# Normalising and transposing four tiles of x in pairs, and moving two pairs of transposes behind a gate and up piece

## The chip, the cores and the metric

The kernel runs on one core of one Trainium2 chip. The metric is device time in microseconds (us) of one execution, median of several. All arithmetic is float32; matrix products are made from float32 values that are split into a high part and a low remainder, three products each.

## The reference, cut to what matters

```python
xn = _layernorm(x, axis=-1)                     # x: 1 x 2048 x 640
s = _A_ref(xn, A_wqkv, A_wo)                    # q, k, v; 32 heads of 20; window of 8 keys, 2 apart; output product
g = _silu(_B_ref(xn, B_w_gate, B_w_up, B_w_down))   # ((xn Wg) * (xn Wu)) Wd, inner width 1536
return x + s * g
```

The layer norm has no weights: `(x - mean) / sqrt(var + 1e-5)` over the 640 columns of a row.

## The kernel before, in words

The 2048 rows are 16 tiles of 128 rows. Tiles 0 to 7 hold the even rows, tiles 8 to 15 the odd rows. Every product needs the normalised x transposed, in `xT`: one buffer per group of four tiles ("chunk" 0 to 3), with a high and a low part.

Tiles 0 to 7 come to it so. `moments` (L180) takes mean and variance of a tile on the vector engine (DVE): two `bn_stats` (L185) and one `bn_aggr` (L186) per tile. `rstd` (L189) makes the scale: a square root on ScalarE (ACT, L191), then a reciprocal and a correction step on DVE. For one or two tiles it works tile by tile (L194 per tile, L195, then L199, L200, L201 per tile); for more tiles it works on all of them at once (L194, L195, L203 to L206). `apply` (L209) subtracts and scales in place, one DVE instruction per tile. `trans` (L218) then makes five 128x128 transposes on TensorE (PE, L223), four into one PSUM bank and one into another; ACT copies each bank out as the high part (L224), and DVE takes the low part from the same bank (L225).

Tiles 8 to 15 have their moments taken from one layout of x (into `mvo`); their scales are made together by `rstd(mvo..., mro...)`; `spread` (L236) distributes means and scales over the partitions with four products `q<-mro,sel` on PE (L240) and one ACT copy (L241). The same x is loaded again in another layout (`load_xq`, L234) into the space of the first, and `trans_odd` (L249) applies norm and transpose on DVE.

`qkv(u, i)` (L283) is one tile's product with one group of heads, 15 matmuls with 300 columns (L292) and two ACT copies. `gate_up(f, ch)` (L384) is one piece of the gated part: 15 matmuls of 512 columns into a bank of tag g, an ACT copy `gs` (L394), 15 into a bank of tag u, and then, as long as no attention is running, an ACT copy `hs` (L407), a GpSimd (POOL) product (L408) and a store. A callback in `amid` is issued between the gate and the up matmuls. Tags g and u have two banks each, tag q has four; the first piece (0,0) is made in two halves of 256 columns.

Nothing reorders the work: the order in which the program records instructions is the order of each engine's queue, and the framework adds the semaphore waits. The order around the change is that of lines 664 to 685: `norm(4, 4)`, `qkv(0, 2)`, `qkv(0, 3)`, the second half of piece (0,0), `trans(4)`, `trans(5)`, `moments(8, 2)`, piece (1,0) with `trans(6)` between gate and up, `moments(10, 2)`, the load of tiles 8 to 11 in the second layout, `trans(7)`, a weight load, `qkv(0, 4)`, `qkv(0, 5)`, `moments(12, 2)`, `moments(14, 2)`, two more loads, the scales of the odd tiles, and piece (0,1) with `spread` between gate and up. On DVE the instructions of these steps stand in just this order; the same holds for ACT. Loads and stores all go through the queue of SyncE (SP).

Of the kernel before, what the change touches and what calls it, by code (L numbers as in the profile page):

```python
# [50 lines left out]
def kernel(  # L51
# [23 lines left out]
    def st(shape, tag, bufs, dt=F32):  # L75
        cnt[0] += 1
        return sb.tile(shape, dt, tag=tag, bufs=bufs, name=f"{tag}_{cnt[0]}")

    def pt(shape, tag, bufs):
        cnt[0] += 1  # L80
        return ps.tile(shape, F32, tag=tag, bufs=bufs, name=f"{tag}_{cnt[0]}")
# [37 lines left out]
    def load_wf(f):  # L119
        wf_raw[f] = st([P, KD, 2, P], "wraw", 3)  # L120
        nc.sync.dma_start(wf_raw[f], wgu[f])
# [49 lines left out]
    def xT_tile(s):  # L171
        if s % TPC == 0:
            y = st([P, 2, KD, CH], "xc", NCH, F32R)
            xT.append((y[:, 0], y[:, 1]))
        hi, lo = xT[s // TPC]
        c = (s % TPC) * P
        return hi[:, :, c:c + P], lo[:, :, c:c + P]


    def moments(s0, n, mv=None):  # L180
        stats = st([P, n, 2, 6], "stats", 2)
        mv = st([P, n, 2], "mv", 2) if mv is None else mv
        for i in range(n):
            for a in range(2):
                nc.vector.bn_stats(stats[:, i, a, :], xt[s0 + i][:, a * HALF:(a + 1) * HALF])  # L185
            nc.vector.bn_aggr(mv[:, i, :], stats[:, i])  # L186
        return mv

    def rstd(var, out, n):  # L189
        r = st([P, 4, NE], "rstd", 2)[:, :, :n]  # L190
        nc.scalar.activation(r[:, 0, :], var, AF.Sqrt, bias=eps_t)  # L191
        step = 1 if n <= 2 else n
        for i in range(0, n, step):
            nc.vector.tensor_scalar_add(r[:, 1, i:i + step], var[:, i:i + step], EPS)  # L194
        nc.vector.reciprocal(r[:, 2, :], r[:, 0, :])  # L195
        if step == 1:
            for i in range(n):
                ve, a, b = (r[:, k, i:i + 1] for k in (1, 2, 3))
                nc.vector.tensor_scalar(b, a, a, ve, op0=ALU.mult, op1=ALU.mult)  # L199
                nc.vector.tensor_scalar(b, b, -0.5, 1.5, op0=ALU.mult, op1=ALU.add)  # L200
                nc.vector.tensor_scalar(out[:, i:i + 1], b, a, None, op0=ALU.mult)  # L201
            return
        nc.vector.tensor_mul(r[:, 3, :], r[:, 2, :], r[:, 2, :])  # L203
        nc.vector.tensor_mul(r[:, 3, :], r[:, 3, :], r[:, 1, :])
        nc.vector.tensor_scalar(r[:, 3, :], r[:, 3, :], -0.5, 1.5, op0=ALU.mult, op1=ALU.add)
        nc.vector.tensor_mul(out, r[:, 3, :], r[:, 2, :])  # L206

    def apply(y, m, r):
        nc.vector.tensor_scalar(y, y, m, r, op0=ALU.subtract, op1=ALU.mult)  # L209

    def norm(s0, n, mv=None):
        mv = moments(s0, n) if mv is None else mv
        r = st([P, n], "r", 2)
        rstd(mv[:, :, 1], r, n)
        for i in range(n):
            apply(xt[s0 + i], mv[:, i, 0:1], r[:, i:i + 1])

    def trans(s, bank=("q", 4)):  # L218
        hi, lo = xT_tile(s)
        for k0, k1 in ((0, 4), (4, KD)):  # L220
            p = pt([P, k1 - k0, P], *(("q", 4) if k0 else bank))
            for k in range(k0, k1):
                nc.tensor.transpose(p[:, k - k0, :], xt[s][:, k * P:(k + 1) * P], ident)  # L223
            nc.scalar.activation(hi[:, k0:k1, :], p, AF.Copy)  # L224
            nc.vector.tensor_sub(lo[:, k0:k1, :], p, hi[:, k0:k1, :].bitcast(F32))  # L225
# [7 lines left out]
    def load_xq(s, n, t):  # L233
        nc.sync.dma_start(t, xq[:, s - NE:s - NE + n, :])  # L234
# [48 lines left out]
    def qkv(u, i, runs=ALL_RUNS, at=None, act=None):  # L283

        g, r = UN[u]
        c = GROUPS[g] * DH
        p = pt([P, 3 * c], "q", 4)
        t0 = (i % TPC) * P
        for n, (a, b, k) in enumerate(runs):
            if n == at:  # L290
                act()
            nc.tensor.matmul(p, xT[(r * NE + i) // TPC][a][:, k, t0:t0 + P], wq[g][b][:, k], start=n == 0,  # L292
                             stop=n == len(runs) - 1, skip_group_check=act is not None)
        nc.scalar.activation(kv_t[u][:, :, W - 1 + i, :], p[:, c:].rearrange("p (a c) -> p a c", a=2), AF.Copy)  # L294
        nc.scalar.activation(q_t[u][:, i, :], p[:, :c], AF.Copy)
        for i0, i1 in ((1, 5), (5, NE)):
            if i == i1 - 1:
                for p0, p1 in ((0, 112), (112, 127)):
                    nc.sync.dma_start(kv_t[u][p0 + 1:p1 + 1, :, i0 - 1:i1 - 1, :],
                                      kv_t[u][p0:p1, :, W - 1 + i0:W - 1 + i1, :])  # L300
# [67 lines left out]
    def advance(budget):  # L368
        credit[0] += budget
        while running and credit[0] > 0:  # L370
            try:
                credit[0] -= next(running[0][1])
            except StopIteration:
                running.pop(0)
        if not running:
            credit[0] = 0
# [4 lines left out]
    def gate_up_half(f, ch, n, p, c=slice(0, CH), **parts):  # L381
        mm3(p[:, c], [([t[:, k, n, :] for t in wf[f]], [t[:, k, c] for t in xT[ch]]) for k in range(KD)], **parts)

    def gate_up(f, ch, between=(), amid=(), part=None):  # L384
        if part is None:
            pp = [pt([P, CH], "g", 2), pt([P, CH], "u", 2)]
            c = slice(0, CH)
        else:
            pp, c = part, slice(CH // 2, CH)
        gate_up_half(f, ch, 0, pp[0], c)  # L390
        for act in amid:
            act()
        gs = st([P, CH], "gs", 2)
        nc.scalar.activation(gs, pp[0], AF.Copy)  # L394
        for act in between:
            act()
        share = (c.stop - c.start) / CH
        finish_piece()
        advance(PACE * 3.25 * share)
        gate_up_half(f, ch, 1, pp[1], c)  # L400

        def finish():
            hs = st([P, CH], "hs", 2)
            if running:
                nc.vector.tensor_mul(hs, pp[1], gs)  # L405
            else:
                nc.scalar.activation(hs, pp[1], AF.Copy)  # L407
                nc.gpsimd.tensor_mul(hs, hs, gs)  # L408
            nc.sync.dma_start(h_scr[ch * TPC:(ch + 1) * TPC, :, f, :].rearrange("t p c -> p t c"),
                              hs.rearrange("p (t c) -> p t c", c=P))  # L410

        unfinished.append(finish)
        if not running:
            finish_piece()
        advance(PACE * 3.25 * share)
# [3 lines left out]
    def finish_piece():  # L419

        while unfinished:
            unfinished.pop(0)()
# [236 lines left out]
    for i in range(NE - 1):  # L659
# [1 line left out]
    sel = st([P, NQ, P], "sel", 1)  # L661
    nc.gpsimd.tensor_copy(sel.rearrange("p q (b i) -> p q b i", i=QB),
                          ident.rearrange("p (q i) -> p q i", i=QB).unsqueeze(2).to_broadcast([P, NQ, NQ, QB]))
    norm(4, 4)
    qkv(0, 2)
    qkv(0, 3)
    gate_up(0, 0, part=part0)
    trans(4)
    trans(5)
    moments(8, 2, mvo[:, 0:2])  # L670
    gate_up(1, 0, amid=(lambda: trans(6),))
    moments(10, 2, mvo[:, 2:4])
    load_xq(8, 4, xc[:, 4:8])
    trans(7)
    load_wf(2)
    qkv(0, 4)
    qkv(0, 5)
# [188 lines left out]
```

## Time and profile before

| what | value |
|---|---|
| time, median of 3 runs | 786.98 us (786.91 to 787.13) |
| time of the profiled execution | 786.92 us |
| its span, first to last instruction | 785.0 us |
| PE matmul busy | 777.6 us, 99% |
| PE weight loads busy | 709.0 us, 90% |
| DVE busy | 661.4 us, 84% |
| ACT busy | 234.4 us, 30% |
| POOL busy | 145.5 us, 19% |

A row of the timeline reads: start in us from the beginning of the span, busy us, engine, line, operation, output tile and input tiles, shape, how many instructions are merged in the row, and in square brackets how long the engine was idle before it and what ended the idle time. PEld rows are weight loads of PE, which run beside its matmuls; SPq rows are issues in SyncE's queue. A merged row has the start of its first instruction and the summed busy time. L12 is line 12 of the kernel. Rows of a table by stretches give the stretch, its length, busy time of each engine with the number of instructions, the clock granted to PE, the share of the DMA engines' time and GB/s.

### The profile page before, as it was taken

To read this page: it belongs to the slowest core of one execution; us is meant where nothing else is said; L and a number is where in the kernel's file an instruction comes from. 1 tells how busy PE (TensorE), PEld (TensorE's weight loads), DVE (VectorE), ACT (ScalarE), POOL (GpSimd) and SP (SyncE) were. 2 spreads that over 40 slices of the span, in tenths; PEclk is the share of its full clock that TensorE was granted. 3 is DMA by queue.
4 is the path that set the end of the run, shared out by engine and by line. 5 is a ranking of instruction groups with operands and counts; after the bars stand their busy time and mean duration, and the time that the engine had idled before them with its cause. 6 is when DMAs were issued, how large, how long until landed. Compare 5 with 4: busy or idle time off the path is not lost.

```text
span 785.0 us, 11221 instructions
## 1 busy us (share of the span) xinstructions
PE 777.6 (99%) x4454; PEld 709.0 (90%) x4454; DVE 661.4 (84%) x660; ACT 234.4 (30%) x536; POOL 145.5 (19%) x110
## 2 busy tenths in 40 slices
PE   8999999999999999999999999999999999999997
PEld 6889898889898898899898989888899999999997
DVE  6989899999999979997999999991278677777775
ACT  4434211121122211311221212012366564444442
POOL 4401212022023100500231000113467600000000
PEclk9999999999999999999999999999999999999999
DMA  9162122141142221404032132332797574555534
GB/s 326 70 223 86 31 70 63 48 123 48 50 113 80 75 71 61 118 27 112 28 113 77 58 86 59 112 96 66 166 262 222 169 268 139 206 201 181 181 101 135
DMA packets 81661, 92.68 MB, mean 118 GB/s; under 512 B 23032, under 2 KB 63304, under 8 KB 81480
## 3 DMA queue, kind: packets, MB, share of 16 engines
q1 hardware_dynamic: 81608, 91.96, 37.9%
q8 instruction: 35, 0.57, 0.3%
q14 instruction: 18, 0.15, 0.1%
HBM read 54.53 MB, written 28.31 MB: 106 GB/s over the span
## 4 chain that ended last, share of the span: by engine, by line
PE 98%; ACT 1%; DMA 1%; DVE 0%; SPq 0%; issue 0%
PE q L292 27%; PE u L95 21%; PE g L95 21%; PE q L605 11%; PE q L95 9%; PE u L605 5%; PE g L605 3%; DMA wraw<-in_wqkv 1%; PE q L223 0%; ACT wf L85 0%; ACT xc L224 0%; SPq L135 0%; DVE t L209 0%; ACT wqh L85 0%; PE q L240 0%
## 5 line engine op out<-in xcount | busy, mean ns | idle before, releaser
L95 PE MATMUL u<-xc,wf 128*128 128x512 f32 (+1 forms) x735 | 176.2, 391 | 0.0
L95 PE MATMUL g<-xc,wf 128*128 128x512 f32 (+1 forms) x735 | 176.2, 391 | 0.0
L95 PEld LDWEIGHTS u<-xc,wf 128*128 128x128 f32 x735 | 135.9, 188 | 32.1
L95 PEld LDWEIGHTS g<-xc,wf 128*128 128x128 f32 x735 | 135.4, 188 | 30.8
L292 PE MATMUL q<-wqh,xc 128*128 128x300 f32 (+1 forms) x960 | 159.8, 310 | 0.9 <-ACT xc L224 0.9
L292 PEld LDWEIGHTS q<-wqh,xc 128*128 128x128 f32 x960 | 146.1, 188 | 2.9 <-ACT xc L224 1.3
L326 DVE TENSOR_TENSOR t<-q,kv 128x1600 f32<-128x1600 f32 (+1 forms) x48 | 98.8, 2058 | 9.6 <-DMA kv<-kv 9.6
L347 DVE TENSOR_TENSOR t<-e,kv 128x1600 f32<-128x1600 f32 (+1 forms) x48 | 96.9, 2037 | 1.1
L86 POOL TENSOR_TENSOR wf<-wraw,wf 128x256 fp32r<-128x256 f32 (+2 forms) x22 | 47.1, 2161 | 253.0 <-ACT wf L85 253.0
L329 DVE TENSOR_REDUCE lg<-t 128x80 f32<-128x1600 f32 (+1 forms) x48 | 92.6, 1930 | 1.2
L394 ACT ACTIVATE gs<-g 128x512 f32<-128x512 f32 x48 | 28.7, 598 | 205.8 <-PE g L95 197.2
L292 PE MATMUL q<-wql,xc 128*128 128x300 f32 (+1 forms) x480 | 86.3, 310 | 0.0
L355 DVE TENSOR_TENSOR t<-t,t 128x1600 f32<-128x1600 f32 (+1 forms) x36 | 78.6, 2184 | 1.1
L292 PEld LDWEIGHTS q<-wql,xc 128*128 128x128 f32 x480 | 74.4, 188 | 0.0
L294 ACT ACTIVATE kv<-q 128x200 f32<-128x200 f32 (+1 forms) x96 | 33.4, 348 | 135.7 <-PE q L292 135.6
L605 PE MATMUL q<-xc,wf 128*128 128x320 f32 x432 | 67.3, 309 | 0.0
L605 PEld LDWEIGHTS q<-xc,wf 128*128 128x128 f32 x432 | 64.3, 188 | 0.0
L86 POOL TENSOR_TENSOR wql<-wraw,wqh 128x300 fp32r<-128x300 f32 (+4 forms) x15 | 33.2, 2239 | 142.5 <-ACT wqh L85 142.5
L95 PE MATMUL q<-wf,wf 128*128 128x320 f32 x156 | 35.7, 311 | 0.0
L405 DVE TENSOR_TENSOR hs<-u,gs 128x512 f32<-128x512 f32 x39 | 26.6, 683 | 0.8 <-issue 0.8
L86 DVE TENSOR_TENSOR wf<-ot,wf 128x640 fp32r<-128x640 f32 x13 | 17.2, 1322 | 12.0 <-ACT wf L85 12.0
L95 PEld LDWEIGHTS q<-wf,wf 128*128 128x128 f32 x156 | 26.1, 189 | 0.0
(169 smaller groups left out, 890.8 us busy)
## 6 DMA issues: line engine op xcount, KB each, us to landing
h_scr<-hs SPq DMA_DIRECT2D x48, 256.0 KB, 2.3
wraw<-in_wgu SPq DMA_DIRECT2D x12, 640.0 KB, 4.9
t<-h_scr SPq DMA_DIRECT2D x8, 768.0 KB, 7.5
hs<-s_scr SPq DMA_DIRECT2D x16, 320.0 KB, 4.0
gs<-in_x SPq DMA_DIRECT2D x16, 320.0 KB, 4.4
wraw<-h_scr SPq DMA_DIRECT2D x12, 384.0 KB, 5.7
out<-q SPq DMA_DIRECT2D x14, 320.0 KB, 3.6
wraw<-in_wd SPq DMA_DIRECT2D x12, 320.0 KB, 4.9
```

The lines of the kernel that those rows point to most:

```text
L86: eng.tensor_sub(lo, raw, hi.bitcast(F32))
L95: nc.tensor.matmul(acc, a, b, start=first and n == 0, stop=last and n == len(runs) - 1)
L292: nc.tensor.matmul(p, xT[(r * NE + i) // TPC][a][:, k, t0:t0 + P], wq[g][b][:, k], start=n == 0, stop=n == len(runs) - 1, skip_group_check ...
L294: nc.scalar.activation(kv_t[u][:, :, W - 1 + i, :], p[:, c:].rearrange("p (a c) -> p a c", a=2), AF.Copy)
L326: nc.vector.tensor_mul(t, q.rearrange("p i c -> p (i c)").unsqueeze(1).to_broadcast([P, 2, NE * c]), places(0, j))
L329: nc.vector.tensor_reduce(out=lg[:, :, j:j + 2].rearrange("p n a -> p a n"), in_=heads(t), op=ALU.add, axis=AX.X)
L347: nc.vector.tensor_mul(heads(t), pw, heads(places(1, j)))
L355: nc.vector.tensor_add(acc, acc, t)
L394: nc.scalar.activation(gs, pp[0], AF.Copy)
L405: nc.vector.tensor_mul(hs, pp[1], gs)
L605: nc.tensor.matmul(p, y[:, i, k], wd_t[name][k][:, l], start=new and r == 0, stop=r == len(runs) - 1, skip_group_check=True)
```

## The change

The norm of tiles 4 to 7 is made in two pairs. `norm(4, 2)` stands where `norm(4, 4)` stood; right behind it come the moments of tiles 6 and 7 (`mv6`); their scales and applies follow behind the transposes of tiles 4 and 5. The pairs take the tile-by-tile branch of `rstd`.

`trans(6)` leaves its place between the gate and the up matmuls of piece (1,0). `trans(6)` and `trans(7)` both stand behind that piece, and their four-block banks are no longer of tag q but the second banks of tags g and u. `moments(10, 2)` and the load of tiles 8 to 11, which stood between piece (1,0) and `trans(7)`, now stand behind `trans(7)`.

```diff
@@ -661,17 +661,20 @@
-    norm(4, 4)
+    norm(4, 2)
+    mv6 = moments(6, 2)
     qkv(0, 2)
     qkv(0, 3)
     gate_up(0, 0, part=part0)
     trans(4)
     trans(5)
+    norm(6, 2, mv6)
     moments(8, 2, mvo[:, 0:2])
-    gate_up(1, 0, amid=(lambda: trans(6),))
+    gate_up(1, 0)
+    trans(6, ("g", 2))
+    trans(7, ("u", 2))
     moments(10, 2, mvo[:, 2:4])
     load_xq(8, 4, xc[:, 4:8])
-    trans(7)
     load_wf(2)
     qkv(0, 4)
     qkv(0, 5)
```

The number of transposes, applies, moments and loads is the same; DVE has twelve more small instructions of one column, as four scales are made in two runs of the tile-by-tile branch (nine instructions each) in place of one run of six, ACT one more square root.

## The prediction

> **What bounds the kernel now.** I read the page first, then what PE waited for, then the timeline of PE, DVE and ACT from 12 to 76 us, where the change lies. First the span and the shares of the chain that ended last, of the page, and then the one wait that PE has after its first 20 us:
>
> ```profile
> span 785.0 us, 11221 instructions
> PE 98%; ACT 1%; DMA 1%; DVE 0%; SPq 0%; issue 0%
> PE q L223 <- PE u L95: 0.4, 1, 0.4
> ```
>
> PE carries 98% of the chain. So whatever delays PE by a microsecond at 30 us delays the end by one, unless something later was waiting for another engine; after this row nothing was. The question is only what PE's stream looks like between 26 and 45 us. This is that stream, from the place with the wait on:
>
> ```profile
> 26.96 1.30 PE L223 MATMUL q<-ident,xc 128*128 128x128 f32 x10 [0.37 <-PE u L95]
> 28.02 3.75 PE L95 MATMUL g<-xc,wf 128*128 128x512 f32 x15
> 31.61 0.71 PE L223 MATMUL q<-ident,xc 128*128 128x128 f32 x5
> 32.07 3.74 PE L95 MATMUL u<-xc,wf 128*128 128x512 f32 x15
> 35.65 0.71 PE L223 MATMUL q<-ident,xc 128*128 128x128 f32 x5
> 36.11 0.39 PE L292 MATMUL q<-wqh,xc 128*128 128x300 f32 x1
> ```
>
> The reader is to see ten transposes of tiles 4 and 5 with 0.37 us of idle PE before them, piece (1,0), cut in two by five transposes, five more, and `qkv(0, 4)` at 36.11. DVE over the same time:
>
> ```profile
> 29.38 1.67 DVE L225 TENSOR_TENSOR xc<-q,xc 128x512 fp32r<-128x512 f32 x4
> 30.97 0.87 DVE L185 BATCH_NORM_STATS2 stats<-xc 128x6 f32<-128x320 f32 x2
> ...
> 33.00 0.83 DVE L225 TENSOR_TENSOR xc<-q,xc 128x512 fp32r<-128x512 f32 x2
> 33.75 0.88 DVE L185 BATCH_NORM_STATS2 stats<-xc 128x6 f32<-128x320 f32 x2
> ...
> 36.97 0.89 DVE L225 TENSOR_TENSOR xc<-q,xc 128x512 fp32r<-128x512 f32 x2 [1.10 <-ACT xc L224]
> 37.77 0.87 DVE L185 BATCH_NORM_STATS2 stats<-t 128x6 f32<-128x320 f32 x2
> ...
> 45.21 1.18 DVE L209 TENSOR_SCALAR xc<-xc,mrq 128x160 f32<-128x160 f32 x4 [1.91 <-DMA xc<-in_xq]
> ```
>
> DVE does the moments of tiles 10 and 11 from 33.75 on, and only then waits 1.10 us for tile 7's transposes; from 37.77 it goes through the moments of tiles 12 to 15 and the odd tiles' scales without a gap. Where that run ends is the row to read most closely:
>
> ```profile
> 42.88 0.65 PEld L95 LDWEIGHTS g<-xc,wf 128*128 128x128 f32 x3
> 42.93 0.17 DVE L205 TENSOR_SCALAR rstd<-rstd 128x8 f32<-128x8 f32 x1
> 43.14 0.17 DVE L206 TENSOR_TENSOR mro<-rstd 128x8 f32<-128x8 f32 x1
> 43.58 1.09 PEld L240 LDWEIGHTS q<-mro,sel 128*128 128x128 f32 x8
> 43.81 0.96 PE L240 MATMUL q<-mro,sel 128*128 128x16 f32 x8
> ```
>
> `mro` is written at 43.14 + 0.17 = 43.31, the gate's last weight loads end at 42.88 + 0.65 = 43.53, and the spread's first load starts at 43.58. DVE arrives 0.2 us before PE needs it. No wait is shown, and there is no slack either: DVE's chain to `mro` is a second critical path that touches PE here.
>
> **The change, part by part.**
>
> *The pairs, at the front (a gain).* From the timeline: the last pair that took the tile-by-tile branch on DVE, the end of tile 5's moments, tile 4's apply, and the weight loads behind it:
>
> ```profile
> 13.47 0.27 DVE L194 TENSOR_SCALAR rstd<-mv 128x1 f32<-128x1 f32 x2
> ...
> 15.44 1.49 DVE L209 TENSOR_SCALAR t<-t,mv,r 128x640 f32<-128x640 f32 x2
> 22.21 0.21 DVE L186 BATCH_NORM_AGGREGATE mv<-stats 128x2 f32<-128x12 f32 x1
> 26.25 0.61 DVE L209 TENSOR_SCALAR xc<-xc,mv,r 128x640 f32<-128x640 f32 x1
> 26.93 1.09 PEld L223 LDWEIGHTS q<-ident,xc 128*128 128x128 f32 x10 [0.55 <-PE u L95]
> ```
>
> Tile 4's apply ended at 26.86 and the transposes' weights started at 26.93: this is what PE's 0.37 us was, although the row names PE. In pairs the nine small scale instructions take 15.44 - 13.47 = 1.97 us but start at 22.42, behind two tiles' moments and not four, so tiles 4 and 5 are ready by 22.42 + 1.97 + 1.49 = 25.9, before PE's 26.6. The gain is between 0.37 (idle of the matmuls) and 0.55 (idle of the weight loads); I take 0.45. The square root moves up in ACT's queue by two microseconds with it and releases the copies of `qkv(0, 2)` behind it earlier, which nobody waited for.
>
> *The second pair (hidden).* Behind tile 5's apply DVE does the moments of tiles 6 and 7 (2.03 for two, as 33.00 - 30.97) to 27.9, four L225 in 30.97 - 29.38 = 1.59 to 29.5, scales in 1.97 and applies in at most 1.49 to 33.0, the moments of tiles 8 and 9 to 35.0. PE wants tile 6 at 34.65 (next), and DVE's next work is there only at 36.0. The twelve extra small instructions thus cost nothing; DVE has one to two microseconds to spare, and the cover is gone only if they cost that much more. ACT's second square root waits for `mv6` (27.9) behind the copies of tile 5, and delays only `gs`, due at 31.
>
> *Transposes of 6 and 7 behind the piece.* Without the cut, gate and up follow each other as later pieces do:
>
> ```profile
> 82.80 3.66 PE L95 MATMUL g<-xc,wf 128*128 128x512 f32 x15
> 86.30 3.67 PE L95 MATMUL u<-xc,wf 128*128 128x512 f32 x15
> ```
>
> That is 3.50 us apart. So: gate at 28.02 - 0.45 = 27.57, up at 31.07, tile 6's transposes 35.65 - 32.07 = 3.58 later at 34.65. Ten transposes joined take about 1.0 (0.46 for five, by 36.11 - 35.65, 1.06 for ten at the front), so `qkv(0, 4)` starts at 35.65, 0.46 earlier than before. Joining saves nothing worth a term: the matmuls are the same. The banks of g and u that they take were last used by tiles 2 and 3 and are long free; the pieces alternate on, and no bank is wanted sooner than before.
>
> *What it does to DVE (the loss).* `moments(10, 2)` used to run while PE did the up matmuls; now it stands in DVE's queue behind tile 7's low parts, which need ACT, which needs PE:
>
> ```profile
> 35.85 0.60 ACT L407 ACTIVATE hs<-u 128x512 f32<-128x512 f32 x1 [2.35 <-PE u L95]
> 36.34 0.76 ACT L224 ACTIVATE xc<-q 128x512 fp32r<-128x512 f32 x2
> ```
>
> Tile 7's transposes stood right behind the up matmuls at 35.65; tile 6's now stand there, at 34.65. So `hs`, the first copy, and DVE's first low part come 1.0 earlier: 34.85, 35.34, 35.97. Now there are two tiles: four low parts, 1.59, end at 37.56. DVE then has the two moments more, 2.03, before the run that it started at 37.77: it starts that run at 39.59, 1.82 later, and `mro` is there at 43.31 + 1.82 = 45.13. The spread's weights can follow 0.07 behind it, as tile 4's did (26.86 to 26.93), or 0.27, as now; I take 45.30. PE comes to the spread 0.46 earlier than before, at 43.12, and waits 2.2 us. The up matmuls of piece (0,1), `qkv(0, 6)` and everything else of PE are queued behind it.
>
> *Sum.* 45.30 - 43.58 = 1.72 us later on PE's chain: -0.46 for the front, +2.18 for the wait. Bounds: with 0.55 at the front, low parts in 1.5 and a handover of 0.07, the same sum gives +1.4; with no gain at the front, +2.3.
>
> *What shifts in SP's queue.* The load of tiles 8 to 11 in the second layout waits for `moments(10, 2)`, now done at 39.6; it holds the weight load and the rest of the queue behind it:
>
> ```profile
> 38.32 0.45 SPq L234 DMA_DIRECT2D xc<-in_xq  x1
> xc<-in_xq SPq DMA_DIRECT2D x1, 1280.0 KB, 6.8
> ```
>
> At 39.6 it lands at 46.4. DVE started the odd tiles at 45.21, 1.6 behind the spread's first load; 1.6 behind 45.30 is 46.9, so the load is in time and costs nothing, and the margin behind it is large:
>
> ```profile
> 67.22 1.72 DVE L258 TENSOR_TENSOR xc<-ot,xc 128x640 fp32r<-128x640 f32 x2
> 73.06 1.53 PE L292 MATMUL q<-wqh,xc 128*128 128x300 f32 x10
> ```
>
> The first of the two low parts (tile 14) ends about 68.0 and is used by the first five of the second row, 5 us later.
>
> *Does a wait of 2.2 us cost PE its clock?* The profile says no for the stretch in which PE waited longest:
>
> ```profile
> 0.00:4.00 4.00, 2.63 (x4) 1.51 (x5) 0.95 (x3) 1.28 (x1) 0.71 (x6) 1.00 0.51 146
> ```
>
> PE was idle for 1.37 of these 4 us and the granted clock is 1.00. No row shows an idle 2.2 us followed by matmuls. [...] If the clock were halved all the same, it is a rival below.
>
> **The time.** The profiled execution took 786.92 us, 0.06 below the median of 786.98. 786.92 + 1.72 = 788.64, so 788.6 us; by the bounds 788.3 to 789.2. What a measurement of this kernel can tell from no change is about 0.2%, 1.6 us: 785.4 to 788.55. The forecast lies just outside.
>
> **Rivals.**
> 1. *The spread does not wait.* If DVE reached `mro` by 43.1, only the front's gain would be left: 786.92 - 0.46 = 786.5. It decides at 2.2 us of DVE time. For it speaks that DVE is idle for 1.10 us before tile 7's low parts now, and less loaded at the front. Against it: that idle time lies ahead of the transposes in both orders, and what stands behind them grows by two moments of fixed length.
> 2. *PE falls to half clock after its wait.* The 3.5 us of the up matmuls would take 7.0: 788.6 + 3.5 = 792.1. Against it the 1.00 above.
> 3. *The second layout lands late.* A load of the same size took 10.4 us at the start:
>
> ```profile
> xc<-in_x SPq DMA_DIRECT2D x1, 1280.0 KB, 10.4
> ```
>
> It would land at 50.0, 3.1 behind the spread, of which the 5 us hide all; only what exceeds 5 is paid, so 2 us more of lateness would be needed for 789 or above.
>
> **Chances.** The forecast's mechanism 0.86, split by its bounds about the line at 788.55: 0.53 above, 0.33 below (its own range 788.2 to 789.3). Rival 1 has 0.06, mostly inside 0.2%; rival 2 has 0.05; rival 3 has 0.03. So slower 0.60, same 0.37, faster 0.03. The range leaves out rivals 1 and 2 and takes in the edges of the first case: 787.6 to 789.8.
>
> **What would show it.** Right: no idle before the transposes at 26.6; gate and up of piece (1,0) 3.5 apart; DVE idle ahead of tile 6's low parts, around 35; `mro` near 45.1; one wait of PE of about 2.2 us at L240 (its line in the changed kernel is the same), released by DVE; from there all rows 1.7 later to the end. Wrong: no idle at L240, or a second wait of PE after it (at the products of the odd tiles or at a gate bank), or a granted clock below 1.00 behind the wait.

## The result and the profile after

The changed kernel took 790.95 us (median of 6 runs, 789.33 to 792.55); the kernel before, beside it, 787.32 (786.91 to 787.76). The ratio is 1.0047, 95% interval 1.0037 to 1.0057: slower by 0.47%, where 0.2% (788.6 us) was forecast and the range ended at 789.8. Two of the six runs (789.33 and 790.18) had a mean granted clock of 0.999; the others had 0.997 (790.65, 791.25) and 0.995 (792.12, 792.55). The profiled execution is the one of 790.65 us: 3.73 above the profiled one of before.

The page of the changed kernel (its profile), and the only wait of PE after 26 us:

```profile
span 788.8 us, 11239 instructions
PE 96%; DVE 2%; ACT 1%; DMA 1%; SPq 0%; issue 0%; ACTq 0%
PE q L240 <- DVE mro L206: 1.7, 1, 1.7
```

DVE has come into the chain through one wait, at the spread. PE's stream in the changed kernel (timeline, 15 to 62 us):

```profile
26.53 1.25 PE L223 MATMUL q<-ident,xc 128*128 128x128 f32 x10
27.55 3.74 PE L95 MATMUL g<-xc,wf 128*128 128x512 f32 x15
31.12 3.66 PE L95 MATMUL u<-xc,wf 128*128 128x512 f32 x15
34.62 0.60 PE L223 MATMUL g<-ident,xc 128*128 128x128 f32 x4
...
35.62 0.94 PE L292 MATMUL q<-wqh,xc 128*128 128x300 f32 x5
...
39.86 3.66 PE L95 MATMUL g<-xc,wf 128*128 128x512 f32 x15
45.21 1.07 PE L240 MATMUL q<-mro,sel 128*128 128x16 f32 x8 [1.69 <-DVE mro L206]
46.13 5.26 PE L95 MATMUL u<-xc,wf 128*128 128x512 f32 x15
51.23 0.85 PE L292 MATMUL q<-wqh,xc 128*128 128x300 f32 x5
```

Up to the row of 46.13 this is the forecast: no idle at 26.5, the piece uncut, transposes at 34.62 (forecast 34.65), the spread at 45.2. The last two rows are not: the up matmuls of piece (0,1) take 51.23 - 46.13 = 5.10 us from start to next start, where they took 48.20 - 44.62 = 3.58 before:

```profile
44.62 3.74 PE L95 MATMUL u<-xc,wf 128*128 128x512 f32 x15
48.20 0.86 PE L292 MATMUL q<-wqh,xc 128*128 128x300 f32 x5
```

DVE in the changed kernel, in the same stretch:

```profile
33.97 0.21 DVE L186 BATCH_NORM_AGGREGATE mvo<-stats 128x2 f32<-128x12 f32 x1
35.93 0.69 DVE L225 TENSOR_TENSOR xc<-g,xc 128x512 fp32r<-128x512 f32 x1 [1.76 <-ACT xc L224]
...
37.53 0.88 DVE L185 BATCH_NORM_STATS2 stats<-xc 128x6 f32<-128x320 f32 x2
...
44.90 0.17 DVE L206 TENSOR_TENSOR mro<-rstd 128x8 f32<-128x8 f32 x1
```

It is idle for 1.76 us ahead of tile 6's low parts, and the moments of tiles 10 and 11 start behind them, at 37.53. `mro` is there at 45.07 (forecast 45.13). Now the same stretch cut by the microsecond; after the length come busy time of PE, PEld, DVE, ACT and POOL, the granted clock, the DMA share and GB/s:

```profile
45.00:46.00 1.00, 0.79 (x8) 0.82 (x8) 0.06 (x1) 0.00 (x0) 0.00 (x0) 1.00 1.00 312
46.00:47.00 1.00, 1.00 (x5) 0.90 (x5) 0.42 (x2) 0.68 (x2) 0.00 (x0) 0.53 0.92 355
47.00:48.00 1.00, 1.00 (x4) 0.71 (x4) 0.97 (x4) 0.03 (x1) 0.00 (x0) 0.50 1.25 347
48.00:49.00 1.00, 1.00 (x4) 0.81 (x3) 1.00 (x3) 0.00 (x0) 0.00 (x0) 0.50 0.97 291
49.00:50.00 1.00, 1.00 (x5) 0.82 (x4) 0.97 (x4) 0.00 (x0) 0.00 (x0) 0.76 0.96 399
```

The clock falls to 0.50 at about 46.06, 0.9 us after PE has gone back to work, and stays there for 0.94 + 1 + 1 + 0.48 = 3.4 us (each row's missing clock, doubled). But the DMA engines are full in the same rows, so from this trace alone the transfers could be the cause. And there is a third part: the delay, 51.23 - 48.20 = 3.03 here, is 3.55 at the last up matmuls before the output products (first row before, second after):

```profile
558.73 3.66 PE L95 MATMUL u<-xc,wf 128*128 128x512 f32 x15
562.28 3.66 PE L95 MATMUL u<-xc,wf 128*128 128x512 f32 x15
```

No wait of PE stands between. The steps of the 300-column products differ instead; two tiles' products, of the kernel before and of the changed one:

```profile
105.18 1.53 PE L292 MATMUL q<-wqh,xc 128*128 128x300 f32 x10
106.55 0.85 PE L292 MATMUL q<-wql,xc 128*128 128x300 f32 x5
107.24 1.53 PE L292 MATMUL q<-wqh,xc 128*128 128x300 f32 x10
```

```profile
108.32 1.55 PE L292 MATMUL q<-wqh,xc 128*128 128x300 f32 x10
109.71 0.85 PE L292 MATMUL q<-wql,xc 128*128 128x300 f32 x5
110.40 1.55 PE L292 MATMUL q<-wqh,xc 128*128 128x300 f32 x10
```

2.06 us a tile before, 2.08 after, at a granted clock of 1.00 in both. So the delay has three parts to be explained: 1.5 us up to the up matmuls, 1.5 in them, and 0.7 in the rest.

### The profile page after: what moved, and what is told of

It is laid out like the page before. It is cut to its first block, busy times and chain, and to the rows that moved or that the text cites. A ratio compares the mean times of both kernels' runs of the same rounds, so it can differ in the third digit from the quotient of the medians.

```text
span 788.8 us, 11239 instructions
## 1 busy us (share of the span) xinstructions
PE 779.9 (99%) x4454; PEld 711.4 (90%) x4454; DVE 661.6 (84%) x672; ACT 235.3 (30%) x537; POOL 146.4 (19%) x110
## 4 chain that ended last, share of the span: by engine, by line
PE 96%; DVE 2%; ACT 1%; DMA 1%; SPq 0%; issue 0%; ACTq 0%
PE q L292 26%; PE u L95 21%; PE g L95 21%; PE q L605 11%; PE q L95 9%; PE u L605 5%; PE g L605 3%; DMA wraw<-in_wqkv 1%; DVE stats L185 1%; PE q L223 0%; SPq L106 0%; DVE xc L225 0%; ACT wf L85 0%; ACT xc L224 0%; DVE mvo L186 0%
## 5 line engine op out<-in xcount | busy, mean ns | idle before, releaser
L86 DVE TENSOR_TENSOR wf<-ot,wf 128x640 fp32r<-128x640 f32 x13 | 15.6, 1199 | 12.8 <-ACT wf L85 12.8
```

Source lines behind the costliest of these rows:

```text
L86: eng.tensor_sub(lo, raw, hi.bitcast(F32))
```

## The experiments

My theory: the two moments behind the transposes make the wait, the wait makes the half clock. Differences below are to the median of the kernel before on the same chip: 787.34 for the first four experiments, 787.05 for the two with the small tiles at their old size and for the first two attempts at a wait of chosen length, 787.15 for the layout alone and the other three waits. Where runs of one kernel fall into two groups by their mean clock, both are given, as "held" (0.999 or 1.000) and "halved" (0.998 or less).

**The two moments ahead of the transposes.**

```diff
     gate_up(1, 0)
+    moments(10, 2, mvo[:, 2:4])
     trans(6, ("g", 2))
     trans(7, ("u", 2))
-    moments(10, 2, mvo[:, 2:4])
```

> The changed kernel with the moments of tiles 10 and 11 ahead of the transposes of tiles 6 and 7 again. My theory (DVE reaches mro 1.6 us late because those two moments stand behind the low parts of tiles 6 and 7, PE waits 1.7 to 2.1 us at the spread, and the granted clock halves for one stretch behind that wait): mro near 43.3 us, no wait of PE over 0.3 us at the spread, clock 1.00 from 44 to 52 us, time 0.2 to 0.5 us below the kernel before. Rival (the loss is in the banks of g and u, or in the pairs): the moments are not the cause, and the time stays 1.5 us or more above the kernel before.

787.43 us in 11 runs, all held: 0.09 above, not 0.2 to 0.5 below; ratio 1.000 (0.9991 to 1.0009). PE does not wait at the spread, which starts at 43.27 (43.81 before), and the clock is 1.00. So the order of these two moments carries wait and half clock both. But the half microsecond that PE is ahead here did not reach the end: the steps of the 300-column products are 2.08 us.

**PE's wait filled with work.**

```diff
-    gate_up(0, 1, amid=(spread,))
+    gate_up(0, 1, amid=(idle_product, idle_product, idle_product, spread))
```

> The changed kernel with three idle products of 384 columns (about 0.64 us each) between the gate and the spread, so that PE works through most of its wait; mro is as late as in the changed kernel. My theory (the loss is the wait, about 1.6 to 1.7 us, and a half clock that the idle time brings on, 1.5 us or more): the spread starts near 45.2 us as in the changed kernel, the clock stays 1.00 from 44 to 52 us, the up matmuls behind take 3.6 us and not 5.1, and the time is 1.5 to 1.9 us above the kernel before, with little spread between runs. Rival (the up matmuls are slowed by the transfers that land beside them, 1.0 of the DMA engines' time from 44 to 48 us): they stay at about 5 us, and the time stays 3 us or more above.

An `idle_product` (L157) multiplies a constant, and nobody reads the result; the profile shows two matmuls for each.

789.37 in 9 runs; the 8 held ones 1.9 above, one halved (791.15), where four of six were halved in the changed kernel. PE's stream:

```profile
43.86 2.10 PE L157 MATMUL q<-ident 128*128 128x384 f32 x6
45.79 0.96 PE L240 MATMUL q<-mro,sel 128*128 128x16 f32 x8
46.60 3.75 PE L95 MATMUL u<-xc,wf 128*128 128x512 f32 x15
50.19 0.85 PE L292 MATMUL q<-wqh,xc 128*128 128x300 f32 x5
```

The spread is as late as in the changed kernel, DMA engines are as busy (1.03 of their time from 44 to 48 us), and the up matmuls take 3.59 at a clock of 1.00. So the transfers do not slow them. What is gone is PE's idle time, and with it the half clock in eight runs of nine.

**The spread behind the piece.**

```diff
-    gate_up(0, 1, amid=(spread,))
+    gate_up(0, 1)
+    spread()
```

> The changed kernel with the spread issued behind the up matmuls of piece (0,1) and not between gate and up: PE comes to it 3.5 us later, DVE is as late as in the changed kernel. My theory: no wait of PE at the spread, clock 1.00, the odd tiles start near 48.4 us and their last low parts are still 1 us or more ahead of PE, time 0.3 to 0.6 us below the kernel before. Rival (the margin of the odd tiles, 5 us before, is used up): PE waits for a low part (L258) at one of the odd tiles' products, and the time is above the kernel before.

789.00 in 11 runs, all held: 1.66 above; ratio 1.0019 (1.0010 to 1.0028). Neither as I expected nor quite as the rival had it. The spread does not wait, but PE does, 20 us later:

```profile
66.28 0.85 PE L292 MATMUL q<-wqh,xc 128*128 128x300 f32 x5
68.01 0.96 PE L292 MATMUL q<-wqh,xc 128*128 128x300 f32 x5 [0.88 <-ACT q L295]
```

```profile
66.85 0.74 ACT L256 ACTIVATE xc<-ot 128x640 fp32r<-128x640 f32 x1 [2.74 <-DVE ot L253]
67.49 0.32 ACT L294 ACTIVATE kv<-q 128x200 f32<-128x200 f32 x1
67.71 0.25 ACT L295 ACTIVATE q<-q 128x100 f32<-128x100 f32 x1
```

Not the low part of an odd tile is late, but a bank: the copies out of the four banks of tag q stand in ACT's queue behind the copy of an odd tile (L256), which waits for DVE. The odd tiles started 2.7 us later here (47.90 against 45.21), with PE 0.65 ahead at 51.68. Two waits followed, with 0.88 and 0.34 us of idle time; by the starts of the rows around them they put PE back 1.7 us in all. In the kernel before, the copies that free these two banks end at 65.75 and 68.43, and PE takes the banks up at 67.56 and 69.62. The real margin is therefore 1.8 us at the first and 1.2 at the second, not the 5 I read from the low parts.

**The move without the pairs.**

```diff
-    norm(4, 2)
-    mv6 = moments(6, 2)
+    norm(4, 4)
...
-    norm(6, 2, mv6)
```

> The kernel before with the transposes of tiles 6 and 7 behind the piece in banks of g and u, and the moments of tiles 10 and 11 behind them, as changed; the norm of tiles 4 to 7 in one run as before. My theory: the move alone carries the loss. PE keeps its 0.4 us of idle time at 26.6 us, mro is 2.0 us later than before (45.2 to 45.6 us), PE waits 1.7 to 2.1 us at the spread, and the time is 1.9 to 2.2 us above the kernel before where the clock holds, 3.5 to 5.5 where it halves. Rival (the pairs, with their twelve more DVE instructions, carry it): within 0.5 us of the kernel before.

790.66 in 6 runs; held (one run) 1.6 above, a little less than forecast, halved (five) 3.5. The profile, halved, has 0.37 us of idle PE at the front, a wait of 1.70 at the spread and up matmuls of 5.13. The move alone carries wait and half clock. And its delay stays at 4.0 us from the first piece behind the spread to the end (0.5 of it is there before the change begins: the second half of piece (0,0) starts at 23.43 in this execution, at 22.93 in that of before, and `mro` comes at 46.06): this kernel loses nothing in the 300-column products. What the pairs change and the move does not is a size: `stats`, `mv` and `r` are made for at most two tiles instead of four. The two buffers of `stats` (12 numbers of 4 bytes for each tile) take 96 bytes less each, and all tiles that are laid out behind them, the weights `wqh` and `wql` among them, stand 192 bytes lower.

**The small tiles at their old size.** First with the moments ahead (the first experiment plus this edit), then the change itself with it:

```diff
-        stats = st([P, n, 2, 6], "stats", 2)
-        mv = st([P, n, 2], "mv", 2) if mv is None else mv
+        stats = st([P, 4, 2, 6], "stats", 2)
+        mv = st([P, 4, 2], "mv", 2)[:, :n] if mv is None else mv
...
-        r = st([P, n], "r", 2)
+        r = st([P, 4], "r", 2)[:, :n]
```

> The changed kernel with the moments of tiles 10 and 11 ahead of the transposes (as e1_moments_first), and with the small tiles stats, mv and r kept at the size for four tiles, so that every later tile of SBUF stands where it stood in the kernel before (in the changed kernel they stand 192 bytes lower). Theory A (the place of the operands costs about 0.5 us: the traces with the pairs lose some 0.1 us in each unit of eight 300-column products up to 340 us, e4_move_only loses nothing): the steps of those products are 2.06 us again and not 2.075, and the time is 0.3 to 0.6 us below the kernel before. Rival (those traces drift for another reason, a chip or a run): the steps stay at 2.075, and the time is that of e1_moments_first, within 0.2 us of the kernel before.

786.82 in 11 runs: 0.23 below; ratio 0.9995 (0.9987 to 1.0004). One of them had a mean clock of 0.998 (787.00) without being longer, and one run in 26 of the kernel before, on the first chip, had it at 789.03; so a single low mean is no proof of this half clock, and the groups below are to be read as groups. The steps are 2.06 again:

```profile
104.58 1.53 PE L292 MATMUL q<-wqh,xc 128*128 128x300 f32 x10
105.95 0.85 PE L292 MATMUL q<-wql,xc 128*128 128x300 f32 x5
106.64 1.53 PE L292 MATMUL q<-wqh,xc 128*128 128x300 f32 x10
```

This has the best median of all, but the interval takes in no change.

> The whole change, with the small tiles stats, mv and r kept at the size for four tiles, so that nothing else in SBUF moves. Theory A: wait and half clock as in the changed kernel, no drift behind them: 1.4 to 1.7 us above the kernel before where the clock holds, 2.9 to 3.3 where it halves for one stretch, and 0.5 us below the changed kernel. Rival: as the changed kernel, 3.0 to 3.8 above.

789.71 in 8 runs: three held, 1.54 above; five halved, 2.85 above. The held runs come near the forecast's sum of 1.72, with nothing beside it. The profile is of a held run, with the same wait as the changed kernel's and the up matmuls at 49.87 - 46.30 = 3.57:

```profile
45.41 1.04 PE L240 MATMUL q<-mro,sel 128*128 128x16 f32 x8 [1.70 <-DVE mro L206]
46.30 3.73 PE L95 MATMUL u<-xc,wf 128*128 128x512 f32 x15
49.87 0.86 PE L292 MATMUL q<-wqh,xc 128*128 128x300 f32 x5
```

**The layout alone, in the kernel before.**

```diff
-        stats = st([P, n, 2, 6], "stats", 2)
-        mv = st([P, n, 2], "mv", 2) if mv is None else mv
+        stats = st([P, n, 2, 6], "stats" if n < 4 else "ot", 2)
+        mv = st([P, n, 2], "mv" if n < 4 else "lg", 2) if mv is None else mv
...
-        r = st([P, n], "r", 2)
+        r = st([P, n], "r" if n < 4 else "lg", 2)
```

> The kernel before, with the small tiles of its norm of four (stats, mv, r) put into tiles of other names that are free then, so that their own shrink as in the changed kernel and all later tiles stand 192 bytes lower, where the changed kernel has them; no instruction is added or moved. Theory A (the place of the operands costs the half microsecond): the steps of the 300-column products are 2.075 us, and the time is 0.4 to 0.8 us above the kernel before. Rival (the drift comes with the pairs' instructions): 2.06 us, same time within 0.2.

787.70 in 11 runs: 0.55 above; ratio 1.0009 (1.0000 to 1.0017), at the edge of what the times alone can tell. The steps are 2.08 us:

```profile
105.37 1.55 PE L292 MATMUL q<-wqh,xc 128*128 128x300 f32 x10
106.75 0.85 PE L292 MATMUL q<-wql,xc 128*128 128x300 f32 x5
107.45 1.55 PE L292 MATMUL q<-wqh,xc 128*128 128x300 f32 x10
```

With the pair above, in which only sizes differ, this settles the third part: it is where the tiles behind `stats` stand, the weights of these products among them. (Here `gs`, `hs`, `ot` and `lg` have changed places as well.) Why 192 bytes matter to these products is open.

**A wait of chosen length, in the kernel before.** DVE work of no use is put ahead of the odd tiles' scales, so that only `mro` is later. The first two attempts, with three such instructions and with six, misfired:

```diff
+    late = st([P, 4, 2, 6], "stats", 2)
+    for _ in range(3):
+        nc.vector.bn_stats(late[:, 0, 0, :], xt[15][:, :HALF])
     nc.vector.tensor_copy(mro[:, 0, :], mvo[:, :, 0])
```

> The kernel before, with three more bn_stats (0.42 us each, results unused) on DVE ahead of the odd tiles' scales, so that mro comes 1.25 us later and PE waits about 1.1 us at the spread; nothing else differs. Theory (the clock falls by how long PE is idle, and the wait of 1.7 to 2.1 us is near the edge, since two runs of the changed kernel in six kept it): clock 1.00 in most runs, 0.9 to 1.2 us above the kernel before. Rival (any wait of a microsecond brings it on, or other things than the wait do): clock 0.997 or 0.998 in most runs and 2.4 us or more above; or no drop here and none with six.

> The kernel before, with six more bn_stats ahead of the odd tiles' scales: mro 2.5 us later, PE waits about 2.3 us at the spread; nothing else differs. Theory: the clock halves for a stretch behind the wait in all or nearly all runs, and the time is 3.8 us above the kernel before, in some runs more. [...]

800.58 and 802.10. The added instructions read tile 15 at a place where its second layout is already being loaded, and so waited for that load, 9.52 us with three; PE was idle for 10.2 and 12.1 us. They say nothing on lengths about 1 to 2 us. What they show is that in these two waits the clock fell to 0.50 long before PE resumed: at 47.6 and 46.26 us in the two profiles, where PE comes back at 54.76 and 56.12. The mean clock was as low in all nine runs (0.989 to 0.993). The mended form reads a constant tile; four instructions are shown, two and six were run as well:

```diff
+    for _ in range(4):
+        nc.vector.bn_stats(late[:, 0, 0, :], sel.rearrange("p q b -> p (q b)")[:, :HALF])
```

> The kernel before, with two unused bn_stats of a constant tile (0.42 us each) on DVE ahead of the odd tiles' scales, the mended form of d3_late and d6_late, whose added reads waited for the load of the second layout. mro near 44.2 us instead of 43.3, PE idle about 0.5 us at the spread. Theory (how long PE is idle decides on the half clock): clock 1.00, 0.5 to 0.8 us above the kernel before. Rival (any wait there brings it on): 2 us or more above in most runs.

> Four such bn_stats: mro near 45.0 us, PE idle about 1.3 us. 1.4 to 1.6 us above the kernel before where the clock holds, about 1.5 more where it halves for a stretch. Theory: near the edge, the clock halves in some runs and not in others, fewer than in the changed kernel (four in six). [...]

> Six such bn_stats: mro near 45.8 us, PE idle about 2.2 us. Theory: the clock halves in all runs or nearly all, 3.5 to 4.5 us above the kernel before. [...]

| added | PE idle before L240 | runs halved | held | halved |
|---|---|---|---|---|
| two | none shown | 0 of 11 | +0.25 | |
| four | 1.03 us | 4 of 7 | +1.4 | +2.8 |
| six | 2.10 us | 4 of 5 | +2.1 | +4.1 |

With two, the half microsecond of wait that I expected did not come: `mro` was there at 44.12, and the spread starts at 44.26 with no wait shown. The profiles with four and with six, both halved:

```profile
45.55 1.04 PE L240 MATMUL q<-mro,sel 128*128 128x16 f32 x8 [1.03 <-DVE mro L206]
46.43 5.28 PE L95 MATMUL u<-xc,wf 128*128 128x512 f32 x15
51.55 0.86 PE L292 MATMUL q<-wqh,xc 128*128 128x300 f32 x5
```

```profile
46.72 1.04 PE L240 MATMUL q<-mro,sel 128*128 128x16 f32 x8 [2.10 <-DVE mro L206]
47.60 5.28 PE L95 MATMUL u<-xc,wf 128*128 128x512 f32 x15
52.72 0.86 PE L292 MATMUL q<-wqh,xc 128*128 128x300 f32 x5
```

Nothing of the change is in these kernels, and the up matmuls take 5.12 us in both. So neither the order nor the banks of the changed kernel are needed; a wait of one microsecond halved the clock in four runs of seven, one of two microseconds in four of five. One of 1.7 (the changed kernel, its same-size form and the move without the pairs) halved it in 14 of 20.

## Why the prediction was wrong

The direction was right, the time was not: the sum ended at +1.72 where the changed kernel is 3.6 above by medians, 3.73 by profiles.

- *The pairs at the front.* Right: taken at 0.45, measured 28.02 - 27.55 = 0.47. Counted from the second half of piece (0,0), which stands ahead of the change (22.93 and 22.98), it is 0.52. That row starts anywhere from 22.77 to 23.48 in the profiles of before, the changed kernel and the first four experiments, so small differences are safer between two rows of one profile than between two profiles.
- *The second pair.* Right: DVE was done with the moments of tile 9 at 34.2, and idle for 1.76 us after it. The twelve instructions cost nothing.
- *What the move does to DVE.* Right in mechanism and size: `mro` at 45.07 (45.13), the spread's weights at 45.18 (45.30). The 0.12 us between are half `mro`, half the handover (0.11 us where I took 0.17). The wait of 2.2 us was worked out from weight loads, which are idle for 2.10 ahead of the spread (row below); the row of the matmuls shows 1.69. With the layout as before and the clock held, the change costs 1.54 us (the same-size form), forecast 1.72.
- *Does a wait of 2.2 us cost PE its clock?* This step failed. It took the answer from 1.37 us of idle at the very start, ahead of PE's first matmul, where the column for the clock reads 1.00, and the rival got 0.05. But by the durations of its instructions PE ran at about half clock there (below the list). In the changed kernel four runs in six had a lower mean clock (0.995 to 0.997), and the profiled one fell to 0.50 behind a wait of 1.69 us. The rival's price was off as well: no run shows the 7.0 us that it gives the up matmuls. Behind waits of 1.0 to 2.1 us the stretch of half clock lasts 3.4 us and the up matmuls take 5.10 to 5.13 us, 1.5 more and not 3.5, as it falls on part of them only. How much idle time brings it on is not shown: 1.03 us was enough in four runs of seven, and about 1.7 us was not in six of 20.
- *A term that was not in the sum.* I took the twelve instructions for all that the pairs change. They also shrink three small tiles, and the operands behind them move by 192 bytes. That costs 0.55 us in the kernel before, about as much as the front gains. Nothing in the profile of before could have sized it, but the diff's new tile sizes could have been named as a risk with both signs.
- *The load of the second layout and the odd tiles.* No cost, as said, but the margin was read in the wrong place: 5 us to the low parts, 1.2 to the banks of tag q through ACT's queue. The change did not come to it; the third experiment did.
- *Rival 1* (no wait) was decided as argued: it is what the order with the moments ahead does.

The weight loads ahead of the spread in the changed kernel, then those of PE's first products in the kernel before:

```profile
45.18 1.00 PEld L240 LDWEIGHTS q<-mro,sel 128*128 128x128 f32 x8 [2.10 <-issue]
```

```profile
4.73 0.34 PEld L157 LDWEIGHTS q<-ident 128*128 128x128 f32 x1 [0.30 <-issue]
5.29 0.19 PEld L157 LDWEIGHTS q<-ident 128*128 128x128 f32 x1 [0.22 <-issue]
```

The single loads from 2.17 to 4.73 us take 0.34 us each, the one at 5.29 takes 0.19. The changed kernel has the same two lengths: loads of this size take 0.19 us from 41 to 43 us, at a clock of 1.00, and 0.33 (median) from 46.6 to 49.4, at 0.50. The products of L157 say the same: they start 0.64 us apart from 2.17 to 4.73, and 0.32 apart in the experiment with the filled wait, where the clock was 1.00. So by these durations PE began at about half clock and came out of it shortly after 5 us, and the 1.00 that the profile gives for 0 to 4 us is not what PE had. To take that 1.00 for a clock that held was a misreading. The trace of before could not say what a wait of 2.2 us does, but it was no evidence that the clock holds.

The parts nearly add up: 1.54 us for the schedule, 0.55 for the layout and 1.3 for one stretch of half clock (2.85 - 1.54, the same-size form) make 3.4 of the measured 3.6. Two runs of the changed kernel had a mean clock of 0.995 and took 792.1 and 792.6, another 1.4 us above those with 0.997. No trace of such a run was taken; whether it is a second stretch is open.

## What to carry to other kernels

When PE carries the whole chain, look for the engines that arrive just ahead of it: a row that shows no wait may still have no slack. Here two moments more in DVE's run up to `mro`, 2.03 us, made `mro` 1.76 us later and PE wait for 1.69. A short wait of PE can cost more than its length: here four runs of seven paid another 1.4 us for 1 us of idle, so an unavoidable wait is worth filling, moving or splitting. Before a clock column is used as evidence, hold it against the durations of equal instructions: it read 1.00 at the start, where they took nearly twice as long. And when a change alters the size of any tile, keep the layout fixed before crediting or blaming the schedule: where a change is worth a fraction of a percent, addresses are a term of their own (0.07% here).

## What the runs showed of the hardware

In the four profiles with a halved clock and waits of 1.0 to 2.1 us the granted clock fell after PE had resumed work, not during the wait: 0.9 us after in the changed kernel and in the move without the pairs, 1.1 with four added instructions, 1.8 with six (spread at 46.72, fall at 48.56). In the two with waits of 10 and 12 us it fell during the wait. It stayed at 0.50 for 3.4 us in the four, and for 13.6 and 17.1 us (47.6 to 61.2, 46.26 to 63.32) in the two: four and five times 3.4. What decides on it is not shown.

In the profiles of before and of the changed kernel the weight loads from 2.17 to 4.73 us take 0.34 and 0.33 us, where loads of this size take 0.19 from 41 to 43 us; the column for the clock reads 1.00 in both places.

The same 15 matmuls with 300 columns took 2.06 or 2.08 us at a granted clock of 1.00 and with the same instructions, by where the tiles behind `stats` stood, their weights among them.
